# A delta-rule attention block with an expert layer: seven products for eight and eleven for twelve one block earlier, the weight sums by ScalarE copies and accumulating DMAs

## The chip, the cores and the metric

The kernel runs on one core of one Trainium2 chip. A core has a matrix engine (TensorE, PE in the profile), a vector engine (VectorE, DVE), an engine for activations (ScalarE, ACT), a general one (GpSimd, POOL), a sequencer that mostly issues transfers (SyncE, SP), and 16 DMA engines that all queues share. Each engine works off its own instructions in order and waits on semaphores for the others. The metric is the device time of one execution, in microseconds; the median over several runs counts.

## The reference

```python
# q, k, v: (4, 8, 768, 48); beta: (4, 8, 768)
k_n = k / (np.linalg.norm(k, axis=-1, keepdims=True) + 1e-06)
for t in range(S):
    y[:, :, t] = np.einsum('bhd,bhde->bhe', q[:, :, t], state)
    v_old = np.einsum('bhde,bhd->bhe', state, kt)
    state = state + bt[:, :, :, None] * np.einsum('bhd,bhe->bhde', kt, vt - v_old)
...
x = attn_out.transpose(0, 2, 1, 3).reshape(3072, 384)
h = x @ w_in                      # (384, 2048)
g = h * np.clip(h + 3.0, 0.0, 6.0) / 6.0
out = g @ w_out                   # (2048, 384)
```

## The kernel before

**Attention.** The 768 tokens are cut into 24 chunks of 32; the four batches stand side by side, so a chunk is 128 rows. For each chunk t there is a preparation (`prep`: POOL scales the keys by their inverse norms into kb, L510; PE turns kb and the queries, L524; ACT copies the turned tile, L532; PE forms the products sc, L547; DVE masks them into L and LB, L558, with masks mb that POOL makes, L486; POOL also makes bkb, L498), the inverse of a triangular matrix for a group of four chunks (`inverse`, the many small DVE operations of L759 and L764, ended by a transposition, L473), and the chain proper (`chain`: ks L806, R L901 and L909, pz and py L827, su L938, the update of the state L956, the output y L843, L819, L863, turned by PE, L873, and copied to xT, L877). `norms` prepares the inverse key norms of a group: squares (ACT for the first groups, POOL from the fourth on, L407 and L409), a DVE reduction each, L413, a root on ACT, L417, and small DVE operations up to L431, whose result L510 waits for.

**Expert layer.** Two chunks make a block of 256 tokens; there are 12 blocks, 0 to 11. For each block `up` forms h from xT and w_in, in 16 pieces of 128 columns of w_in, three matmuls of 256 columns each (L994), and ACT (L1001) and DVE (L1004) make g of each. `down` forms out from g and w_out: 32 matmuls of 384 columns (L1162) for a block.

From a certain block on, two cheaper schemes stand in for these. `down_by_seven` (from block `FIRST` = 2) cuts the matrices into quarters and forms out with seven products of quarters for eight (56 matmuls of 192 columns, L1226, in `product`); it needs sums of quarters of w_out (T1, T2, T4 in the tile `spare`, and a changed quarter B12 of w_out itself) and, per block, sums of quarters of g on DVE (L1212), copies of products on ACT (L1233) and additions on POOL (L1236). `up_by_eleven` (from block `UF` = 3) forms h with eleven products for twelve (L1066, nine matmuls for each of eight pieces, of 128 and 256 columns). It needs sums of quarters of w_in (S1, S2, S4 in the tile `sums_in`, and a changed W21 in w_in itself), sums of quarters of xT on DVE (`token_sums`, L1056), and additions on POOL (L1030) and DVE (L1093, L1097) to put g together.

**Sums of weights before.** `quarters` makes T1, T2 and T4 by twelve DVE operations (L1197), one at a time between other work, after the weights have been converted from their double-precision form (`convert`, last step L389); `last_quarter` changes B12 by four DVE operations (L1203) during `up` of block 2, drawn by `mlp_units`; `weight_sums` makes S1, S2, S4 and W21 by sixteen POOL operations (L1030) during `down` of block 1 and after.

**Order.** The first part is issued from a list of words, `ORDER`, written out by hand: each word takes the next step of a generator (`c` takes one of `convert` and then `quarters`; `u` one unit of the expert layer; `gu` one pending L1004; `n9` a step of the norms; `p9` of the preparation of chunk 9). After the list a loop over chunks takes a plan of 15 units a chunk; each unit takes one step of `mlp_units` and the attention's steps that the plan puts there. A block is 16 units of `up` and 16 of `down` (14 of `down_by_seven`). The order in which instructions are issued is the order on each engine's queue. PSUM tiles are handed out from a ring of four (`pm`) and one of two (`pc`), so a tile's last reader stands ahead of its next writer. The output tile o has one buffer.

SP issues the loads of keys, queries and values and the stores of o. POOL issues no DMA before the change.

Of the kernel before, what the change touches and what calls it, by code (L numbers as in the profile page):

```python
# [38 lines left out]
ru c i2 u*2 i2 gu i2*3 q i2*5 y4 h4 n9 i2 e*2 n9*2 i2*4 q i2 y4 e n9 u ru i2*3 u i2 ru*2 gu h4 u n9  # L39
i2*2 u i2 e i2*6 y4 u k n9*3 u gu i2 y4 n9 i2 p9 q i2*2 gu  # L40
# [4 lines left out]
def kernel(  # L45
# [21 lines left out]
    nc = tc.nc  # L67
# [950 lines left out]
    UF = 3  # L1018
# [13 lines left out]
    def weight_sums():  # L1032
        for j in range(0, NPR, 2):
            r = slice(j, j + 2)
            plus_minus(S1[:, r], W21[:, r], W22[:, r], ALU.add)
            yield
            plus_minus(S2[:, r], S1[:, r], W11[:, r], ALU.subtract)
            yield
            plus_minus(S4[:, r], W12[:, r], S2[:, r], ALU.subtract)
            yield  # L1040
            plus_minus(W21[:, r], W11[:, r], W21[:, r], ALU.subtract)
            yield
# [5 lines left out]
    def token_sums(blk):  # L1048
# [6 lines left out]
        for out, a, b in ((T1x, B12, B11), (T2x, B22, T1x), (B12, B22, B12), (T4x, B21, T2x)):  # L1055
            nc.vector.tensor_tensor(out=out, in0=a, in1=b, op=ALU.subtract)  # L1056
# [129 lines left out]
    FIRST = 2  # L1186
# [6 lines left out]
    def quarters():  # L1193

        for o, a, b in ((T1, B12, B11), (T2, B22, T1), (T4, T2, B21)):
            for f in range(0, HF, 2):
                nc.vector.tensor_tensor(  # L1197
                    out=o[:, f : f + 2], in0=a[:, f : f + 2], in1=b[:, f : f + 2], op=ALU.subtract
                )
                yield  # L1200

    def last_quarter(f):
        nc.vector.tensor_tensor(  # L1203
            out=B12[:, f : f + 2], in0=B22[:, f : f + 2], in1=B12[:, f : f + 2], op=ALU.subtract
        )

    def down_by_seven(blk):
# [12 lines left out]
        def product(n, a, b, half):  # L1220

            if half == 0:
                ring("pm", NPM, ("po", blk, "by", n))
                ps[n] = psM.tile([128, HM], FP32, name="po", tag=slot["pm"])
            for f in range(half * HF // 2, (half + 1) * HF // 2):
# [14 lines left out]
        settle()  # L1240
# [4 lines left out]
        yield  # L1245
        product(4, A22, T4, 0)
        yield
        product(4, A22, T4, 1)
        copy(C21, 4, -1.0)
        sums(ALU.add, A22, A21, A22, lo)  # L1250
        yield
        product(2, A12, B21, 0)
        sums(ALU.add, A22, A21, A22, hi)
        yield
        product(2, A12, B21, 1)
        copy(C11, 2)
# [6 lines left out]
        copy(C22, 5)  # L1263
# [33 lines left out]
    def mlp_units():  # L1297
# [10 lines left out]
        def downs(blk):  # L1308
            if blk >= FIRST:
                yield from down_by_seven(blk)  # L1310
                return
# [253 lines left out]
```

## Time and profile before

| what | us |
|---|---|
| median of three runs | 661.96 |
| lowest, highest | 661.61, 663.02 |
| span of the profiled execution | 660.3 |
| product of block 1 (`down`), start to end on PE | 148.07 to 178.76 |
| `up` of block 2 | 178.76 to 205.69 |
| seven products of block 2 | 205.69 to 230.00 |
| eleven products of block 3 | 230.00 to 255.78 |

The profile is of one execution, whose span is 1.7 us under the median. In timelines the first column is the start from the span's beginning and the second how long the piece took; a matmul in single precision leaves two records, so `x8` of L1162 is four matmuls. The bracket at the end is idle time of the engine before the piece and what ended it. In a table of windows the columns are length, then busy time and count of PE, PE's weight loads, DVE, ACT and POOL, the granted clock, the share of DMA and GB/s. The costliest groups of the expert layer:

```
L1066 PE MATMUL ph<-xT,w_in 128*128 128x128 f32 (+1 forms) x720 | 156.8, 321 | 0.0
L1226 PE MATMUL po<-w_out,g 128*128 128x192 f32 x640 | 110.6, 326 | 0.0
L994 PE MATMUL ph<-xT,w_in 128*128 128x128 f32 (+1 forms) x384 | 72.0, 338 | 0.6 <-ACT xT L877 0.6
L1162 PE MATMUL po<-w_out,g 128*128 128x384 f32 x128 | 45.4, 490 | 0.0
```

Columns: line, engine, operation, names, shapes, count; busy time and mean nanoseconds of one; idle time of the engine before them.

### The profile page before, as it was taken

What the parts mean: (1) busy time and instruction counts of PE and PEld (TensorE: products, weight loads), DVE (VectorE), ACT (ScalarE), POOL (GpSimd) and SP (SyncE); (2) the same over time, 40 slices, a digit from 0 to 9 for tenths busy, and PEclk for the clock granted to TensorE, in tenths of its full rate; (3) what the DMA queues carried; (4) which work ended last, traced back from release to release, by engine and by line L of the source; (5) the groups of instructions that cost most, each with busy time, mean ns of one, the idle gap of its engine ahead of it and who ended that gap; (6) DMA issues with size and microseconds to landing.
All of it is one profiled execution on the core that took longest, in us unless ns stands there. A gap on an engine that the chain in (4) does not pass through costs nothing.

```text
span 660.3 us, 26640 instructions
## 1 busy us (share of the span) xinstructions
PE 632.5 (96%) x11640; PEld 569.2 (86%) x11640; DVE 499.2 (76%) x1170; ACT 282.3 (43%) x548; POOL 225.1 (34%) x352
## 2 busy tenths in 40 slices
PE   2768999999999999999999999999999999999997
PEld 2658987776689989999999999999999999999997
DVE  5899877798657988758988848979658998456354
ACT  5887689332243154154154244244244144153250
POOL 6531022003661353553254354164051242331430
PEclk9998999999999999999999999999999999999999
DMA  7888346202040030041030030020020020000000
GB/s 174 204 198 235 77 102 164 51 25 43 9 87 18 3 74 3 3 90 22 3 74 3 2 74 3 2 63 2 3 50 2 3 49 3 23 18 2 26 1 24
DMA packets 88692, 33.28 MB, mean 50 GB/s; under 512 B 80224, under 2 KB 83424, under 8 KB 88576
## 3 DMA queue, kind: packets, MB, share of 16 engines
q1 hardware_dynamic: 88224, 31.29, 20.8%
q8 instruction: 91, 1.49, 0.9%
q10 hardware_dynamic: 352, 0.30, 0.2%
q14 instruction: 25, 0.20, 0.1%
HBM read 26.84 MB, written 4.72 MB: 48 GB/s over the span
## 4 chain that ended last, share of the span: by engine, by line
PE 91%; DVE 3%; DMA 2%; SPq 1%; ACT 1%; issue 1%; DVEq 0%
PE po L1226 28%; PE ph L1066 27%; PE ph L994 9%; PE po L1162 6%; PE ks L806 4%; PE su L938 3%; PE pt L524 3%; PE pz L827 3%; PE py L827 3%; PE sc L547 2%; PE yt L873 1%; DMA spare<-in_moe_w_in_dram 1%; PE pi L684 1%; DMA w_out<-in_moe_w_in_dram 1%; SPq L168 1%
## 5 line engine op out<-in xcount | busy, mean ns | idle before, releaser
L1066 PE MATMUL ph<-xT,w_in 128*128 128x128 f32 (+1 forms) x720 | 156.8, 321 | 0.0
L1030 POOL TENSOR_TENSOR g<-g 128x256 f32<-128x256 f32 (+1 forms) x144 | 88.6, 616 | 104.7 <-ACT g L1080 99.1
L1066 PEld LDWEIGHTS ph<-xT,w_in 128*128 128x128 f32 x720 | 116.8, 191 | 6.7
L1226 PE MATMUL po<-w_out,g 128*128 128x192 f32 x640 | 110.6, 326 | 0.0
L1226 PEld LDWEIGHTS po<-w_out,g 128*128 128x128 f32 x640 | 104.6, 190 | 0.5
L1080 ACT ACTIVATE g<-ph 128x512 f32<-128x512 f32 x72 | 43.1, 598 | 105.1 <-PE ph L1066 105.1
L1226 PE MATMUL po<-spare,g 128*128 128x192 f32 x480 | 86.7, 332 | 0.0
L1226 PEld LDWEIGHTS po<-spare,g 128*128 128x128 f32 x480 | 77.2, 190 | 1.8
L994 PE MATMUL ph<-xT,w_in 128*128 128x128 f32 (+1 forms) x384 | 72.0, 338 | 0.6 <-ACT xT L877 0.6
L1236 POOL TENSOR_TENSOR o<-o,u 128x192 f32<-128x192 f32 x18 | 13.3, 739 | 163.8 <-ACT o L1233 86.6
L994 PEld LDWEIGHTS ph<-xT,w_in 128*128 128x128 f32 x384 | 59.6, 195 | 7.7 <-ACT xT L877 0.8
L1093 DVE TENSOR_TENSOR g<-ph,g 128x256 f32<-128x256 f32 x72 | 30.2, 419 | 46.8 <-PE ph L1066 33.5
L759 DVE TENSOR_TENSOR pr<-A 128x30 f32<-128x30 f32 (+9 forms) x150 | 57.3, 382 | 3.3
L1212 DVE TENSOR_TENSOR g<-g 128x512 f32<-128x512 f32 x80 | 56.1, 722 | 3.5 <-PE po L1226 3.5
L1113 DVE SCALAR_TENSOR_TENSOR g<-o,g 128x512 f32<-128x512 f32 x72 | 52.6, 730 | 7.8 <-ACT o L1110 7.7
L764 DVE TENSOR_TENSOR A<-A,pr 128x30 f32<-128x30 f32 (+9 forms) x150 | 55.1, 367 | 3.3
L1110 ACT ACTIVATE o<-g,halves 128x512 f32<-128x512 f32 x72 | 52.2, 725 | 11.3 <-DVE g L1113 8.4
L1066 PE MATMUL ph<-beta_tok,sums_in 128*128 128x128 f32 x288 | 55.9, 275 | 0.0
L356 ACT ACTIVATE spare<-spare,places 128x768 uint16<-128x768 uint16 (+1 forms) x56 | 52.8, 947 | 3.2 <-DMA kf<-in_k_dram 1.6
L1233 ACT ACTIVATE o<-po 128x192 f32<-128x192 f32 x40 | 13.3, 332 | 82.7 <-PE po L1226 79.2
L510 POOL TENSOR_TENSOR kb<-kf,inv 128x384 f32<-128x384 f32 x24 | 21.7, 907 | 75.5 <-issue 43.1
L1162 PE MATMUL po<-w_out,g 128*128 128x384 f32 x128 | 45.4, 490 | 0.0
(141 smaller groups left out, 1019.1 us busy)
## 6 DMA issues: line engine op xcount, KB each, us to landing
kf<-in_k_dram SPq DMA_DIRECT2D x96, 48.0 KB, 2.6
qb<-in_q_dram SPq DMA_DIRECT2D x96, 48.0 KB, 2.4
vf<-in_v_dram SPq DMA_DIRECT2D x96, 48.0 KB, 2.1
out_dram<-o SPq DMA_DIRECT2D x90, 48.0 KB, 1.6
spare<-in_moe_w_in_dram SPq DMA_DIRECT2D x4, 768.0 KB, 6.6
w_out<-in_moe_w_in_dram SPq DMA_DIRECT2D x4, 768.0 KB, 6.1
w_out<-in_moe_w_out_dram SPq DMA_DIRECT2D x4, 768.0 KB, 5.8
spare<-in_moe_w_out_dram SPq DMA_DIRECT2D x4, 768.0 KB, 5.2
```

The lines of the kernel that those rows point to most:

```text
L356: nc.scalar.activation(out=z, in_=z if n else d.bitcast(I16)[:, :, :, 3], func=func, bias=places[:, n : n + 1], scale=scale,)
L759: nc.vector.tensor_tensor(out=pv, in0=A[:, j + 1 :, j].unsqueeze(2).to_broadcast([n, w, j]), in1=A[:, j, 0:j].unsqueeze(1).to_broadcast([n ...
L764: nc.vector.tensor_tensor(out=A[:, j + 1 :, 0:j], in0=A[:, j + 1 :, 0:j], in1=pv, op=ALU.subtract)
L994: nc.tensor.matmul(ph[:, cols], lhsT=w_in[:, s, f * 128 : (f + 1) * 128], rhs=xT[:, s, cols], start=(s == 0), stop=(s == NKT - 1),)
L1030: nc.gpsimd.tensor_tensor(out=out, in0=a, in1=b, op=op)
L1066: nc.tensor.matmul(ph[:, n], lhsT=w, rhs=x, start=start, stop=stop, skip_group_check=True)
L1080: nc.scalar.activation(out=gt, in_=ph[:], func=ACTF.Copy)
L1110: nc.scalar.activation(out=r, in_=g, func=ACTF.Relu, bias=half, scale=1.0 / 6.0)
L1113: nc.vector.scalar_tensor_tensor(out=g, in0=r, scalar=1.0, in1=g, op0=ALU.min, op1=ALU.mult)
L1162: nc.tensor.matmul(pos[c][:], lhsT=gs[blk, f // 2][:, f % 2, c * P : (c + 1) * P], rhs=w_out[:, f, :], start=(f == 0), stop=(f == NFC - 1),)
L1212: nc.vector.tensor_tensor(out=A(f, *out, 4), in0=A(f, *a, 4), in1=A(f, *b, 4), op=op)
L1226: nc.tensor.matmul(ps[n][:], lhsT=A(f - f % 2, *a)[:, f % 2], rhs=b[:, f], start=(f == 0), stop=(f == HF - 1),)
```

## The change

`FIRST` goes from 2 to 1 and `UF` from 3 to 2: block 1's product with w_out is made by seven products, block 2's with w_in by eleven. All sums of weights are made in another way: ACT copies one operand (with scale -1 where a sign is wanted, `minus`), and a DMA issued from POOL's queue adds the other one into it (`plus_by_dma`). Signs of some sums change so that every second step is an addition: T1 is B11 - B12, T1x is B11 - B12, and product 5 is copied with -1. T4 no longer goes through T2: it takes -B21, then B22, then T1. B12 and W21 are negated in place by ACT and then added to. In block 1 the order of the seven products is 1, 2, 4, 5, 7, 6, 3, with product 2 in four parts, so that the block has 16 units as before; in the other blocks it stays 1, 4, 2, 5, 7, 6, 3. Some `gu` and `c` words of `ORDER` move. The loop's branch for an ordinary `down` after block 0 goes.

There are nine such DMAs: T1, T4, T2 and T4 again (768 KB each), S1 (512 KB), B12 (768 KB), W21, S2 and S4 (512 KB each). On POOL's queue they stand, in this order, T1, T4, T2, T4, S1 and B12 ahead of kb (L510) and the masks of one chunk, W21 and S2 ahead of the next kb, bkb and masks, and S4, after one addition to o, ahead of the four L409. On ACT's queue the copies T1, T4 and T2 stand ahead of an L407 and the two evictions of block 0's po, and W21, S1 and B12 ahead of the root L417, S2 and S4 behind the copy of product 1.

```diff
-    UF = 3
+    UF = 2
...
     def weight_sums():
-        for j in range(0, NPR, 2):
-            r = slice(j, j + 2)
-            plus_minus(S1[:, r], W21[:, r], W22[:, r], ALU.add)
-            yield
...
+        minus(W21, W21)
+        minus(S1, W22)
+        yield
+        plus_by_dma(S1, W21)
+        nc.scalar.activation(out=S2, in_=W11, func=ACTF.Copy)
+        nc.scalar.activation(out=S4, in_=W12, func=ACTF.Copy)
+        for _ in range(4):
+            yield
+        plus_by_dma(W21, W11)
+        plus_by_dma(S2, S1)
+        for _ in range(4):
+            yield
+        plus_by_dma(S4, S2)
+        yield
...
-    FIRST = 2
+    FIRST = 1
...
     def quarters():
-        for o, a, b in ((T1, B12, B11), (T2, B22, T1), (T4, T2, B21)):
-            for f in range(0, HF, 2):
-                nc.vector.tensor_tensor(
-                    out=o[:, f : f + 2], in0=a[:, f : f + 2], in1=b[:, f : f + 2], op=ALU.subtract
-                )
-                yield
+        minus(T1, B12)
+        minus(T4, B21)
+        yield
+        plus_by_dma(T1, B11)
+        plus_by_dma(T4, B22)
+        nc.scalar.activation(out=T2, in_=B22, func=ACTF.Copy)
+        yield
+        plus_by_dma(T2, T1)
+        plus_by_dma(T4, T1)
+        past.add("quarters")
+        yield
+
+    def minus(out, a):
+        nc.scalar.activation(out=out, in_=a, func=ACTF.Copy, scale=-1.0)
+
+    def plus_by_dma(out, a):
+        nc.gpsimd.dma_start(out=out, in_=a, accum_op=ALU.add)
+
+    def last_quarter():
+        minus(B12, B12)
+        yield
+        plus_by_dma(B12, B22)
+        yield
...
+        if blk == FIRST:
+            for part in range(4):
+                product(2, A12, B21, part, 4)
+                if part == 3:
+                    copy(C11, 2)
+                yield
+            needs("quarters")
         product(4, A22, T4, 0)
...
-            for _ in downs(blk):
-                next(sums, None)
+            for n, _ in enumerate(down_by_seven(blk)):
                 next(sums, None)
+                if blk == FIRST:
+                    next(b12, None)
                 yield
```

More of the change, by code (lines that the diff above doesn't have):

```diff
@@ L1307, in mlp_units @@
                 yield
[L1308 to L1311, printed above, removed]
[L1312 to L1317 removed]
+        b12 = last_quarter()
         for blk in range(1, N // CB):
```

60 lines of the change are left out of this document (25 added, 35 removed).

## The prediction

> **What bounds the kernel now.** I read the page first, for the engine that the chain of waits runs through, then the stages that the change touches, and then each engine's timeline around them.
>
> ```profile
> PE 632.5 (96%) x11640; PEld 569.2 (86%) x11640; DVE 499.2 (76%) x1170; ACT 282.3 (43%) x548; POOL 225.1 (34%) x352
> PE 91%; DVE 3%; DMA 2%; SPq 1%; ACT 1%; issue 1%; DVEq 0%
> ```
>
> TensorE (PE) is the bound: 91% of the chain is its own work, and no other engine is near full over the span. So every matmul that goes from the dense part comes off the end, and every wait put before a matmul there goes on it. The stages by windows (the ordinary product of block one, the ordinary `up` of block two, the seven products of block two, the eleven of block three):
>
> ```profile
> 148.07:178.76 30.69, 30.69 (x543) 20.00 (x542) 23.50 (x58) 7.37 (x15) 13.57 (x17) 1.00 0.12 25
> 178.76:205.69 26.93, 26.93 (x433) 23.14 (x428) 17.70 (x42) 9.60 (x20) 15.05 (x21) 1.00 0.36 69
> 205.69:230.00 24.31, 24.31 (x444) 23.24 (x443) 20.69 (x48) 4.79 (x11) 4.57 (x7) 1.00 0.01 2
> 230.00:255.78 25.78, 25.78 (x478) 23.41 (x477) 21.43 (x53) 12.85 (x26) 14.51 (x23) 1.00 0.24 49
> ```
>
> The first figure after the length is PE's busy time: it equals the length, so PE never waits here. What feeds PE in these stages stands in the timelines; these lines of PE, DVE, POOL and ACT carry the argument:
>
> ```profile
> 148.06 2.74 PE L1162 MATMUL po<-w_out,g 128*128 128x384 f32 x8
> 156.12 0.60 PE L524 MATMUL pt<-ident,kb 128*128 128x128 f32 x4
> 169.78 0.89 PE L938 MATMUL su<-R,bkb 32*64 32x48 f32 x64
> ```
>
> ```profile
> 154.41 0.35 DVE L431 RECIPROCAL inv<-nt 128x32 f32<-128x32 f32 x1
> 168.37 0.41 DVE L558 TENSOR_TENSOR LB<-sc,mb 128x256 f32<-128x256 f32 x1
> ```
>
> ```profile
> 154.89 0.83 POOL L510 TENSOR_TENSOR kb<-kf,inv 128x384 f32<-128x384 f32 x1 [43.06 <-issue]
> 164.97 0.82 POOL L409 TENSOR_TENSOR sq<-kf 128x384 f32<-128x384 f32 x1
> ```
>
> ```profile
> 140.35 0.51 ACT L407 ACTIVATE sq<-kf 128x384 f32<-128x384 f32 x1
> ```
>
> Two chains end close to PE. The norm chain: DVE's L431 at 154.41 lets POOL make kb (done 155.72), and PE turns kb at 156.12, 0.4 us later. The square chain: POOL's first L409 at 164.97 starts four squares and their DVE reductions in turn; DVE runs L558 between them (ends 168.78) and PE's su, which needs it, comes at 169.78, 1.0 us later.
>
> **The change part by part.** All times are on the clock of the trace before.
>
> *Matmuls.* Eight records of 384 columns (two a matmul) take 148.06 to 150.65, 0.65 us a matmul; 32 of them are 20.7 us. The last block's 56 matmuls of 192 columns take 18.2 us. So the product of block one loses 2.5 us of PE. The `up` stage of 26.93 us becomes one like those of eleven, 25.78 (230.00 to 255.78) and 25.58 (280.08 to 305.66): 1.25 us less. Together 3.75 us, if nothing waits.
>
> *The norm chain.* DVE is busy without a gap from 130 to 156, so block one's matmuls don't set when L431 comes. It comes later: one more L1004 (0.34 us) stands ahead of it, and ACT's three copies T1, T4, T2 stand ahead of the L407 of 140.35. A copy of 1536 costs 1.46 us (0.60 for 512 and 0.33 for 192 give 0.84 ns an element), three 4.2: that L407 ends at 145.1, its reduction on DVE starts at 145.15 instead of 144.62, 0.5 us later. So L431 starts at 155.3, kb ends at 156.5, and PE, which would be there at 154.4 (0.25 us of that for po's buffers, evicted later behind the same copies), waits until 156.55. The wait eats 2.1 us of the 2.5; after it only one short piece (half of product 2's last half, 0.65 us) is still to be won. The other ACT copies (W21, S1, B12, S2, S4: 1.03, 1.03, 1.46, 1.03, 1.03) run to 154.7; the ACT work behind them, root for L420 (152.3, wanted at 154.4) and the xT eviction, has cover.
>
> *The removed sums.* DVE's twelve L1197 and four L1203 (0.5 to 0.9 us each) and POOL's sixteen `sums_in`/`w_in` operations (0.73) go, DVE gains eight L1212 (0.69) and POOL sixteen L1030 on g and five L1236. PE waited for none of them, and waits for none now: nothing.
>
> *Nine accumulating DMAs on POOL's queue.* In POOL's order: T1, T4 (first pass), T2, T4 (second), S1, B12, then kb and mb, W21, S2, then kb, bkb, mb, one L1236, S4, then the four L409. An issue waits on POOL for what it reads, so T2 waits for T1's landing, second T4 for the first, W21 for S1, S4 for S2, and everything behind waits too. The trace has no POOL DMA and no accumulation. Their price is bounded by plain packets:
>
> ```profile
> spare<-in_moe_w_out_dram SPq DMA_DIRECT2D x4, 768.0 KB, 5.2
> out_dram<-o SPq DMA_DIRECT2D x90, 48.0 KB, 1.6
> ```
>
> The packet records give 121 ns for 3072 bytes, 25 bytes/ns an engine, 16 engines: 768 KB (T's and B12) move in 1.95 us, 512 KB (S's, W21) in 1.3. A 48 KB store whose bytes take 0.1 us lands after 1.6, so 1.5 is fixed. One end is this plain price; the other is twice the bytes, since each sum reads its destination as well as its source through the same engines. I take twice, 3.9 and 2.6: two plain packets are the nearest rows to two operands read. By 36 ns for a 768-byte packet, the pieces of T1, T4 and B12, it is 4.6 for those: the upper end.
>
> The Trainium skill, Collectives: The Full Stack, section The bandwidth ceiling, says that a reduction by DMA runs at half a copy's rate because it needs two source reads (its ratio 1.93). No run here shows it yet; by 1.93 instead of 2 the 27.3 us of movement below shrink by 1.0 us, and the sum would be 664.9.
>
> On one queue, one behind the other: T1 issues at 142.0 (its ACT copy's end), moves to 145.9, lands 147.4; T4 to 149.8, lands 151.3; T2 to 153.7; second T4 (issued 151.3) to 157.6, lands 159.1; S1 (151.7) to 160.2, lands 161.7; B12 to 164.1, lands 165.6; W21 (161.7) to 166.7; S2 to 169.3, lands 170.8. PE wants T4 at 158.1 (156.55 and 0.44 + 0.65 + 0.44): 1.0 us of wait. B12 is wanted at 167.6: no wait. But S4 is issued only at 170.8, and takes POOL 0.4 (the SP's issue of 768 KB, 385 to 452 ns, is the nearest row). So the first L409 starts at 171.2, not 164.97; 3.8 us later (as 164.97 to 168.78) L558 ends, at 175.0, and su starts 5.2 us later than before.
>
> *Sum.* From su on PE runs as before, then wins 1.25 in the eleven: 660.3 + 5.2 - 1.25 = 664.3 for a profiled execution. The median of the runs shown lies 1.65 above its span (661.96 against 660.3): **665.9 us**, slower by 0.6%. With 4.6 for the pieces of 768 bytes and the same doubling for 512-byte ones (26 ns between the records of 192 and 768 bytes, so 3.3) S2 lands at 174.3, su starts 8.8 late: 669.5. With 1.75 times the plain price S2 lands at 167.4, su is 1.8 late: 662.5. So the forecast's own range is 662.5 to 669.5; it decides from the factor at which S2 lands after 165.7, where POOL would get to S4 anyway: about 1.65.
>
> **The rivals.**
>
> *The sums move at the plain rate* (the second read hides beside the write). Then T4 lands at 151.3 and S2 at 162.1 (at 1.5 times still at 163.9), before POOL gets to S4 at 165.7 (L558's end at 163.7, mb 1.4, L1236 0.6). The square chain starts at 166.1, su at 169.9, 0.1 late; the eleven gives 1.25: 660.8, not slower, at the edge of what can be told. For it: DMA is only 0.12 busy in this stage, while the 5.2 us of the plain row were taken under the load of the first 120 us. Against: each byte written is two to read.
>
> *All 3.75 us are won*: 658.2. It needs the norm chain 2 us earlier; against it stands DVE without a gap up to 156. For it, PE is all there is on the chain afterwards.
>
> *POOL's issuing is the price*, not the bytes. T1, T4, S1, B12 and W21 are 1024 pieces each. If POOL makes pieces at the pace of its elements (0.73 us for 256, L1030) that is 2.9 us each: S1 issues from 151.0 to 153.9, B12 to 156.8, kb ends at 157.6 and PE turns it 1.1 late; W21 and S2 then push POOL's S4 to 166.9 and, with plain bytes, su to 171.1, 1.3 late, less 1.25: 662.0, no change.
>
> **How the numbers follow.** Forecast 0.45; plain rate 0.30; all won 0.12; issuing 0.08; 0.05 for what I don't see, mostly slower. About 0.2%, 1.3 us, is what a measurement can tell, so faster is under 660.6: all won and a little over half of the plain rate, 0.30. Same: the rest of the plain rate and the issuing, 0.17. Slower 0.53. The range that holds all but 2 in 10 runs from 658.0 (all won) to 670.5 (the dear packets and a microsecond): cases of both signs, beside the 662.5 to 669.5 of the likeliest.
>
> **What would show it.** In the profile after: PE idle before kb's transpose (about 2 us, released by POOL's L510), before product 4 (1 us, by the DMA into `spare`), and most before su (5 us, released by L558, POOL's L409 behind the last accumulating DMA). The DMA section gives the landing of 768 KB: near 3.5 us says plain, 5.5 and over twice. If POOL's own rows of these DMAs are long, it is the issuing. A span under 658 would make the norm chain wrong; landings of 10 us and more would make it far slower than I say.

## The result, and the profile after

| what | before | after |
|---|---|---|
| median of four runs each, us | 662.36 | 685.53 |
| lowest to highest | 661.61 to 663.02 | 681.11 to 685.95 |
| span of the profiled execution | 660.3 | 683.8 |
| su behind the ordinary or new product of block one, start | 169.78 | 187.85 |
| `up` or eleven of block two, length | 26.93 | 26.22 |

The change makes the kernel slower, by a ratio of 1.0335 (95% interval 1.0306 to 1.0365). The forecast was 665.9, with a range up to 670.5: the side was right, the size was not. The page of the changed kernel, its busy time of PE and its chain of waits:

```profile
PE 635.3 (93%) x11736; PEld 580.4 (85%) x11736; DVE 501.2 (73%) x1176; ACT 295.2 (43%) x567; POOL 236.9 (35%) x366
PE 86%; DMA 5%; DVE 3%; POOL 2%; SPq 1%; issue 1%; ACT 1%; POOLq 0%; DVEq 0%
```

PE's share of the chain fell from 91 to 86%, and POOL, which was not on it, is there with 2%. Where PE stands still is told by its timeline. These are its waits between 140 and 275 us that last over 0.5 us; all but the last end in a line that the change touches or feeds:

```profile
151.76 1.57 PE L1246 MATMUL po<-w_out,g 128*128 128x192 f32 x8 [0.81 <-DVE g L1004]
162.84 1.11 PE L524 MATMUL pt<-ident,kb 128*128 128x128 f32 x4 [7.58 <-POOL kb L510]
174.38 0.66 PE L524 MATMUL pt<-ident,kb 128*128 128x128 f32 x4 [1.52 <-POOL kb L510]
187.85 1.19 PE L938 MATMUL su<-R,bkb 32*64 32x48 f32 x60 [7.17 <-DVE LB L558]
269.35 0.31 PE L827 MATMUL py<-R,LB 32*32 32x48 f32 x9 [1.68 <-issue]
```

The kb of 162.84 and the su of 187.85 (60 of its 64 records; four stand ahead of the wait) are two of the three places that the forecast named, with 2.1 and 5.2 us; at the third, product 4, PE does not wait. The last line is of another kind: PE stops in the middle of a group of small matmuls, and nothing in the profile releases it. What keeps POOL from kb and from the squares is in its own timeline:

```profile
141.89 3.31 POOL L1219 DMA_DIRECT2D spare<-w_out  x2 [30.32 <-ACT spare L1216]
151.08 0.89 POOL L1219 DMA_DIRECT2D spare<-spare  x1 [5.88 <-ACT sums_in L1216]
157.93 0.85 POOL L1219 DMA_DIRECT2D spare<-spare  x1 [5.96 <-DMA spare<-w_out]
158.48 1.89 POOL L1219 DMA_DIRECT2D sums_in<-w_in  x1
159.38 2.55 POOL L1219 DMA_DIRECT2D w_out<-w_out  x1
160.29 2.49 POOL L510 TENSOR_TENSOR kb<-kf,inv 128x384 f32<-128x384 f32 x1
170.99 1.56 POOL L1219 DMA_DIRECT2D w_in<-w_in  x1 [7.07 <-PE pz L827]
182.87 0.86 POOL L1219 DMA_DIRECT2D sums_in<-sums_in  x1 [6.08 <-DMA sums_in<-sums_in]
183.49 1.10 POOL L409 TENSOR_TENSOR sq<-kf 128x384 f32<-128x384 f32 x1
```

In order: T1 and T4, T2, T4's second pass, S1, B12, kb, W21 (S2 stands right behind it), S4, the first square. The bracket of W21 names a PE instruction, but S1's landing, at 170.45 by its semaphore, is what it stood for. From 151.97 to 157.93 POOL stands at T4's second pass, until the first has landed (157.64); kb was ready to be made at 155.1. From 176.78 to 182.87 it stands at S4, until S2 has landed (182.58), and the squares stand behind it. The issues themselves take some 0.9 us where rows are whole (each partition's bytes lie in one piece) and some 1.6 where they are cut into pieces of 768 or 512 bytes. Rows of queued POOL work overlap, so the time from the end of one to the end of the next is what counts: T4's, S1's and B12's end at 158.8, 160.4 and 161.9, and kb's at 162.8. The DMA section gives the landings:

```profile
spare<-w_out POOLq DMA_DIRECT2D x2, 768.0 KB, 11.5
spare<-spare POOLq DMA_DIRECT2D x2, 768.0 KB, 9.3
sums_in<-sums_in POOLq DMA_DIRECT2D x2, 512.0 KB, 7.6
w_out<-w_out POOLq DMA_DIRECT2D x1, 768.0 KB, 17.7
sums_in<-w_in POOLq DMA_DIRECT2D x1, 512.0 KB, 12.0
w_in<-w_in POOLq DMA_DIRECT2D x1, 512.0 KB, 9.1
```

These contain the time in the queue. From 144.18, when the first byte moves, to 182.22, when S2's last one does, the queue is never empty for over 0.1 us: by the packets' own times, 16 engines need 37.2 us for the first eight sums, where the forecast had 27.3. Last, the windows of four stages and stretches (length; busy time and count of PE, its weight loads, DVE, ACT and POOL; granted clock; share of DMA; GB/s):

```profile
147.85:198.37 50.52, 33.34 (x592) 30.17 (x591) 23.93 (x61) 12.97 (x23) 22.81 (x27) 0.83 0.83 129
198.37:224.59 26.22, 26.05 (x481) 23.77 (x477) 16.65 (x40) 12.93 (x26) 14.05 (x23) 1.00 0.40 76
187.85:191.60 3.75, 3.75 (x128) 3.54 (x129) 3.03 (x6) 0.32 (x1) 2.66 (x4) 0.50 0.02 4
270.10:273.50 3.40, 3.40 (x15) 3.21 (x15) 1.09 (x3) 1.49 (x3) 1.18 (x2) 0.50 0.02 5
```

The stage of block one's product takes 50.52 us for 30.69, with 17.2 us of it idle. The two last windows are stretches in which PE works at half its clock: the granted clock is 0.50 from 184.77, within the wait before su, to 191.59, and from 270.10, 0.8 us behind the pause at 269, to 273.51 (and from 157.46 to 167.70 around the wait before kb). So the 23.5 us between the two spans add up from the end that counts: su starts 18.1 later; 3.75 us at clock 0.50 behind it cost 1.9; the eleven of block two gives back 0.7; the pause of 1.68 at 269 and the 3.40 us at half clock behind it cost 3.4, and another such pause, 1.02 us at 315, makes 23.7. The two waits before kb are not in this sum: S2's landing sets su, and they lie in front of it.

### The profile page after: what moved, and what is told of

It is laid out like the page before. It is cut to its first block, busy times and chain, and to the rows that moved or that the text cites. A ratio compares the mean times of both kernels' runs of the same rounds, so it can differ in the third digit from the quotient of the medians.

```text
span 683.8 us, 26908 instructions
## 1 busy us (share of the span) xinstructions
PE 635.3 (93%) x11736; PEld 580.4 (85%) x11736; DVE 501.2 (73%) x1176; ACT 295.2 (43%) x567; POOL 236.9 (35%) x366
## 4 chain that ended last, share of the span: by engine, by line
PE 86%; DMA 5%; DVE 3%; POOL 2%; SPq 1%; issue 1%; ACT 1%; POOLq 0%; DVEq 0%
PE ph L1074 29%; PE po L1246 29%; PE ph L994 6%; PE pt L524 3%; PE ks L806 3%; PE po L1170 3%; PE su L938 3%; PE py L827 3%; PE pz L827 3%; PE sc L547 2%; DMA sums_in<-sums_in 2%; PE yt L873 1%; DMA out_dram<-o 1%; DMA w_out<-in_moe_w_in_dram 1%; DMA spare<-in_moe_w_in_dram 1%
## 5 line engine op out<-in xcount | busy, mean ns | idle before, releaser
L1030 POOL TENSOR_TENSOR g<-g 128x256 f32<-128x256 f32 (+1 forms) x160 | 97.8, 612 | 123.1 <-ACT g L1088 116.8
L1246 PE MATMUL po<-w_out,g 128*128 128x192 f32 x704 | 123.1, 328 | 0.8 <-DVE g L1004 0.8
L1246 PEld LDWEIGHTS po<-w_out,g 128*128 128x128 f32 x704 | 115.4, 191 | 1.9 <-DVE g L1004 1.1
L1246 PE MATMUL po<-spare,g 128*128 128x192 f32 x528 | 96.8, 335 | 0.1
L1246 PEld LDWEIGHTS po<-spare,g 128*128 128x128 f32 x528 | 86.2, 192 | 2.5 <-ACT o L1253 0.5
L1232 DVE TENSOR_TENSOR g<-g 128x512 f32<-128x512 f32 x88 | 61.8, 723 | 12.3 <-PE po L1246 12.3
L1121 DVE SCALAR_TENSOR_TENSOR g<-o,g 128x512 f32<-128x512 f32 x80 | 58.7, 733 | 8.9 <-ACT o L1118 8.9
L1118 ACT ACTIVATE o<-g,halves 128x512 f32<-128x512 f32 x80 | 57.8, 723 | 12.9 <-DVE g L1121 9.7
L1074 PE MATMUL ph<-beta_tok,sums_in 128*128 128x128 f32 x320 | 62.2, 276 | 0.0
L759 DVE TENSOR_TENSOR pr<-A 128x30 f32<-128x30 f32 (+9 forms) x150 | 58.4, 389 | 3.6
L764 DVE TENSOR_TENSOR A<-A,pr 128x30 f32<-128x30 f32 (+9 forms) x150 | 53.2, 355 | 3.1
L1074 PEld LDWEIGHTS ph<-beta_tok,sums_in 128*128 128x128 f32 x320 | 48.8, 193 | 0.0
L532 ACT ACTIVATE KQ<-pt 128x512 f32<-128x512 f32 x48 | 28.2, 598 | 34.7 <-PE pt L524 33.8
```

The source lines that it names most:

```text
L759: nc.vector.tensor_tensor(out=pv, in0=A[:, j + 1 :, j].unsqueeze(2).to_broadcast([n, w, j]), in1=A[:, j, 0:j].unsqueeze(1).to_broadcast([n ...
L764: nc.vector.tensor_tensor(out=A[:, j + 1 :, 0:j], in0=A[:, j + 1 :, 0:j], in1=pv, op=ALU.subtract)
L1030: nc.gpsimd.tensor_tensor(out=out, in0=a, in1=b, op=op)
L1074: nc.tensor.matmul(ph[:, n], lhsT=w, rhs=x, start=start, stop=stop, skip_group_check=True)
L1118: nc.scalar.activation(out=r, in_=g, func=ACTF.Relu, bias=half, scale=1.0 / 6.0)
L1121: nc.vector.scalar_tensor_tensor(out=g, in0=r, scalar=1.0, in1=g, op0=ALU.min, op1=ALU.mult)
```

## The experiments

Kernels that differ only from 140 us on (on PE's queue from 148) still reach the same su at different times, between 144.3 and 148.5: it is the fifth su of the profile, at 144.3 in the changed kernel and 144.6 before, and the expectations call it chunk 5. So beside the median a "tail" is given: the span less the start of that su. It is 515.7 before and 539.5 after, good to 0.1 us. A tail is of one execution; how much it varies between executions of one kernel was not measured.

**One half of the change at a time.** The first kernel takes `weight_sums` and `token_sums` of the change and UF = 2, with FIRST = 2 and the sums of w_out on DVE (cut where dots stand, as in all edits here):

```diff
-    UF = 3
+    UF = 2
...
-            plus_minus(S1[:, r], W21[:, r], W22[:, r], ALU.add)
+        plus_by_dma(S1, W21)
```

> Kernel before with block two's product with w_in by eleven and the four sums of w_in by ScalarE copies and accumulating DMAs; block one's product with w_out stays ordinary and its sums stay on VectorE. Theory (each accumulating DMA moves slowly, 4.2 us for 512 KB in 512-byte pieces and 2.8 in whole rows, and they move one behind the other): with an empty queue ahead S1 lands near 156, S2 near 167, POOL comes to S4 only 0 to 2 us late, so at most 2 us of wait before su and none before kb's transposition beyond 1 us: 661 to 664 us. Rival (POOL's own time for issuing, 0.9 to 1.7 us a DMA, is the price): the same 4 of 9 issues stand ahead of the same work, so 4/9 of the loss of 23 us, near 672. Rival (whatever runs beside the DMAs gets slower): the DMAs move 2 of 5.9 MB, near 670.

The second is the changed kernel with UF = 3 and `weight_sums` and `token_sums` as before:

```diff
-    UF = 2
+    UF = 3
```

> Changed kernel with block two's product with w_in made in the ordinary way again and the sums of w_in by POOL operations in block two; the five accumulating DMAs of w_out and the seven products of block one stay. Theory: T4 still lands near 157.6, POOL still stands at the second T4 until then, kb ends near 161 and PE waits some 6 us before kb's transposition, then runs about 3 us at half clock; no S2, so no wait before su: 662.4 - 2.5 + 6 + 2 = 668, 666 to 671. If e1 is near 662 and this near 668, the two halves together (685.5) cost 17 us more than the sum of both, because S1, W21 and S2 stand behind w_out's DMAs. Rival (POOL's issuing): 5/9 of 23 us, near 675.

Measured: 672.7 (671.2 to 675.0) and 673.0 us (671.5 to 674.7), ratios 1.0141 (1.0100 to 1.0181) and 1.0143 (1.0104 to 1.0182); tails 525.5 and 524.8. Both miss high, and both medians lie near what the rival of POOL's issuing gave (672 and 675); the waits show another cause. PE's timeline, with w_in alone and with w_out alone:

```profile
178.38 1.19 PE L938 MATMUL su<-R,bkb 32*64 32x48 f32 x60 [3.06 <-DVE LB L558]
```

```profile
163.45 1.12 PE L524 MATMUL pt<-ident,kb 128*128 128x128 f32 x4 [6.02 <-POOL kb L510]
```

With w_in alone S1 lands at 161.30 and S2 11.7 us later, at 172.97; POOL stands at S4 for 5.4 us until then, and su waits 3.1. A pause of 1.9 comes in a group of sc, and PE works 5.7 us at half clock. With w_out alone PE waits 6.0 before kb and 1.7 at product 4, and works 3.2 us at half clock. The halves cost 9.8 and 9.1 in the tail, together 18.9, of the whole 23.8: 4.9 us more than their sum, and not the 17 that were expected.

**What of the DMA is dear.** First the same bytes in whole rows:

```diff
-        plus_by_dma(T1, B11)
-        plus_by_dma(T4, B22)
+        plus_by_dma(T1, w_out[:, 0:4])
+        plus_by_dma(T4, w_out[:, 8:12])
...
-        plus_by_dma(S1, W21)
+        plus_by_dma(S1, w_in[:, 0, 1024:2048])
```

(and W21 and B12 likewise).

> Changed kernel; the accumulating DMAs T1, T4, B12, S1, W21 take the same number of bytes, but from and to whole stretches of 6144 or 4096 bytes a partition instead of 768- or 512-byte pieces. That adds other parts of the weights than the sums need (T1, T4, B12, S1, W21 get other values). Theory (small pieces cost 84 ns for 768 bytes and 65 for 512, against 530 for 6144 and 340 for 4096): 768 KB take 4.2 us instead of 5.7, 512 KB 2.8 instead of 4.2; T4 lands near 154.8, S2 near 174.5; the wait before kb shrinks from 7.6 to 4 us, that before su from 7.2 to 2 to 3, less time at half clock: near 675, 672 to 678. If the price went by bytes alone: 685. If all small-piece cost were the loss: under 668.

Then plain copies:

```diff
-        nc.gpsimd.dma_start(out=out, in_=a, accum_op=ALU.add)
+        nc.gpsimd.dma_start(out=out, in_=a)
```

> Changed kernel, its nine DMAs as plain copies on the same queue, in the same order and with the same pieces; nothing is added, so T1, T2, T4, B12, S1, S2, S4, W21 hold one operand instead of a sum. Theory (it is the accumulation in the DMA engines that moves slowly): a 768-byte piece takes 36 to 45 ns instead of 84 to 91, T4 lands by 150, S2 by 166, no wait over 1.5 us before kb or su: 661 to 664. Rival (POOL's issuing, 0.9 to 1.7 us a DMA, or its waiting on one landing after another, whatever the kind): 680 or more. Rival (any SBUF to SBUF transfer is as slow): 680 or more with pieces at 80 ns.

Measured: whole rows 681.4 us (ratio 1.0262, 1.0217 to 1.0307; tail 534.7), plain copies 666.65 (1.0065, 1.0039 to 1.0090; tail 521.5). The number of issues and their order on POOL's queue are the same in all three, so 19 of the 23 us come with the accumulation. Part of this is POOL's time: the issue of a cut DMA takes it 1.6 us with accumulation and 0.9 as a plain copy, that of whole rows 0.9 and 0.55. The packets' records, means:

```
                          bytes   ns      768 or 512 KB take
changed   cut rows, 768     768   90.9    5.8 us
          cut rows, 512     512   66.4    4.2
          whole rows       6144   529     4.2
          whole rows       4096   343     2.7
plain     six of 768       4608   236     2.5
          whole rows       6144   259     2.1
          rows and eights of 512
                           4096   204     1.6
```

Accumulating costs 1.7 to 2.0 times a plain copy in whole rows and 2.3 to 2.6 times in cut ones: by the sizes of the packets, a plain copy packs six pieces of 768 bytes or eight of 512 into one, an accumulation moves each by itself. Whole rows bring T4 down to 154.63 and S2 to 177.24, but PE still waits 2.2 before kb, 3.0 at product 4 and 5.2 before su, and the pause at 265 with its half clock stays, so less comes back than expected. With plain copies the two waits are nearly as the rival of the forecast had them. The landings are later than it said: T4's second pass lands at 158.69 for 151.3 and S2 at 168.42 for 162.1, and only 1.8 us of each is this profile's later fifth su.

```profile
spare<-w_out POOLq DMA_DIRECT2D x2, 768.0 KB, 6.3
spare<-spare POOLq DMA_DIRECT2D x2, 768.0 KB, 5.4
w_out<-w_out POOLq DMA_DIRECT2D x1, 768.0 KB, 8.7
```

```profile
158.16 0.66 PE L524 MATMUL pt<-ident,kb 128*128 128x128 f32 x4 [0.86 <-POOL kb L510]
169.21 0.83 PE L547 MATMUL sc<-KQ 64*32 64x64 f32 x62 [1.20 <-issue]
173.44 0.97 PE L938 MATMUL su<-R,bkb 32*64 32x48 f32 x60 [0.36 <-DVE LB L558]
```

(DMA section and PE's timeline of the kernel with plain copies.) Both waits are under a microsecond. Its tail is 5.8 us over that of the kernel before, and three pauses of the kind without a releaser make 5.6 of it: 1.20 here, 1.94 at 254 with 1.7 lost at half clock behind it, and 0.73 at 300.

**The pauses.** They were counted in PE's instructions: matmuls, weight loads (a single-precision matmul is two of each) and the few that only wait for a semaphore. The 18 profiles of this study leave 58 pauses of over 0.25 us, past 60 us of the span, without a releaser. All lie at 193 or 194 modulo 256, and in each case a 16 KB packet on the queue of kind `instruction` began 2.2 to 2.9 us before PE went on. The changed kernel has 92 such packets for 23671 instructions of PE, one for 256. Over all 18 traces PE goes past such a count 1638 times with a packet before it, and never sooner than 2.16 us after the packet for it (counts and packets taken in order) began. To move them, small matmuls into a tile that is overwritten were put at the start of PE's program, four instructions each:

```diff
             pt = psM.tile([128, NP, P], FP32, name="pt", tag=slot["pm"])
+            for _ in range(14 if t == 0 and j == 0 else 0):
+                nc.tensor.matmul(
+                    pt[0:32, 0, 0:64], lhsT=ident[0:64, 0:32], rhs=ident[0:64, 0:64], start=True, stop=True
+                )
```

A first try used `lhsT=ident[:]` and `rhs=ident[:, 0:32]` into 128 rows:

> Changed kernel with 14 small matmuls more at the very start of TensorE's program, where it waits for its first keys. A single-precision matmul is four instructions there, so all that follows stands 56 instructions later. In the runs so far every pause of TensorE that nothing in the profile explains came when 193 or 194 instructions modulo 256 had been issued (1.68 us at 269, 1.02 us at 315 in the changed kernel). Theory (code is loaded in blocks of 256 instructions, and a block that holds two bursts of small attention matmuls is used up before the next is there): the shift takes the block's border out of those bursts; both pauses go, and with the first the 3.4 us at half clock behind it: 685.5 - 1.7 - 1.0 - 1.7 = 681, 679 to 683. Rival (the pauses hang on data or on transfers beside): unchanged, 685.

> Kernel before with 50 small matmuls more at the very start of TensorE's program, 200 instructions, as many as block one's and block two's new products add in the changed kernel (201). Theory of code blocks: the borders then fall in the later chunks where they fall in the changed kernel, and pauses of 1 to 2 us come there, with or without a stretch at half clock: 664 to 667. Rival (pauses hang on the DMAs or the waits of the changed kernel): 662.5, no change; the 50 matmuls lie in TensorE's idle start.

then the form above, 14 in the changed kernel and 50 in the kernel before:

> As the kernel with 56 instructions more, but with 14 matmuls of 64 rows and 64 columns, which are over before the first keys are there (in the first try each of the 14 took 0.2 us and held up the start). Theory of code blocks: from chunk 5 on the same gain as there, 4.1 us (535.4 from that point to the end, against 539.5 in the changed kernel): 681.4 us, 680 to 683. Rival: 685.5.

> Kernel before with 200 instructions more at the start, in matmuls of 64 rows and 64 columns that are over before the first keys are there. Theory of code blocks: two pauses, 1.6 us in a burst near 250 and 1.1 near 295, as in the first try (518.7 us from chunk 5 to the end against 515.7): 662.4 + 3.0 = 665.4, 664.5 to 667.5, with up to 1.7 more if the first is followed by half clock. Rival: 662.5, no change.

Measured: 692.0 and 684.2 us in the first form, 691.4 (ratio 1.0436, 1.0409 to 1.0462) and 674.3 (1.0153, 1.0124 to 1.0183) in the second. None of the four medians came out as expected. A matmul took 0.43 us in the first form and 0.22 in the second, not the 0.2 of the expectation, so 50 of them run 15.4 and 4.7 us past the first keys (8.1) and hold up the start; 14 do not. But in the changed kernel 56 instructions put borders into groups of small matmuls in the first 110 us: in the second form pauses of 1.57 and 2.93 come at 87 and 106, and the fifth su at 154.7 for 144.3. The tails are as expected in both forms: 535.4 and 534.9 for the changed kernel (539.5 without), 518.7 and 518.7 for the kernel before (515.7 without). In the kernel before, which has no such pause past 60 us, 200 instructions bring two behind the fifth su, at the same counts as in the changed one (PE's timeline, second form):

```profile
259.42 0.29 PE L831 MATMUL py<-R,LB 32*32 32x48 f32 x9 [1.62 <-issue]
303.95 0.30 PE L551 MATMUL sc<-KQ 64*32 64x64 f32 x2 [1.04 <-issue]
```

So these pauses belong to the place in the program, not to the DMAs: the change adds 201 instructions and takes them on itself, 4.4 us with the half clock. The Trainium skill, Runtime: NRT & Kernel Launch, section Instruction fetch mechanics, has code come in blocks of 16 KiB, 256 instructions, by the sequencer's own DMA, and the cost of crossing a border "mostly hidden". Block and packet agree with the rows above; hidden it was not in the 58 pauses, of up to 3.4 us. Two groups of 64 small matmuls at a border do not always bring one: in the kernel before, su and py from 397.2 to 398.8 fill a whole block without one; the next block's packet had begun 2.5 us before its border. That the loading makes the pause is inferred from the counts, the packets and the 2.16 us; why a packet begins late was not looked into.

The kernel with plain copies and 56 instructions more:

> The kernel with plain copies in the place of the accumulating DMAs (T1, T2, T4, B12, S1, S2, S4, W21 hold one operand), with 56 instructions more at the start. Theory: what plain copies still lost (5.8 us from chunk 5 on) is all code blocks, 1.9 and 1.2 and 0.7 us of pauses and 1.7 at half clock; with the borders moved 661 to 662.5 is left, the forecast's own price for the plain rate (660.8). Rival (nine DMAs on POOL's queue cost some us even at the plain rate): 664 and more.

Measured 673.2 us, ratio 1.0151 (1.0129 to 1.0173): the early pauses again (fifth su at 154.3). Its tail is 518.3, 3.2 less than without and 2.6 over the kernel before; pauses of 0.36 and 0.26 and waits of 0.87 before kb, 1.33 at product 5 (for DVE's sums of g, L1236) and 0.97 before su are in it. So even with landings as early as a plain copy's the change did not reach the 515.7 less 3.75 that its matmuls promise: by the tail the rival is nearer than the theory.

**Half clock.** The wait before kb was filled with work, 33 matmuls of 128 columns into the tile that the transposition overwrites, and 31 small ones at the start make up a full block:

```diff
+            if t == 9 and j == 0:
+                for n in range(33):
+                    nc.tensor.matmul(
+                        pt[:, n % NP], lhsT=ident[:], rhs=w_in[:, 2, 0:128], start=True, stop=True
+                    )
```

> Changed kernel with 33 matmuls of 128 columns, into the tile that kb's transposition then overwrites, ahead of the transposition that waits 7.6 us, so that TensorE is busy in that wait; and 31 small ones at the start, so that 256 instructions are added in all and code borders stay where they were from there on. Theory (the wait costs twice: the idle time, and then a clock of 0.5 until 167.7): the clock stays at 1.00 through 157 to 168, the 4.9 us that TensorE worked at half clock become 2.5 shorter: 683, 682 to 684, with the wait itself (until kb, 162.8) unchanged and the pauses at 269 and 315 still there. Rival (the half clock costs nothing because the next thing, S2, sets the time anyway): su still starts at 187.9 and the time stays at 685.5.

Measured 697.6 us, ratio 1.0521 (1.0498 to 1.0545), with the start held up as above (fifth su at 160.7); tail 536.5. The clock stays at 1.00 up to kb, but PE then waits for T4 at product 4 and for S2's landing before su (PE's timeline):

```profile
182.66 4.52 PE L1256 MATMUL po<-spare,g 128*128 128x192 f32 x16 [2.09 <-DMA spare<-spare]
203.87 1.19 PE L948 MATMUL su<-R,bkb 32*64 32x48 f32 x60 [6.00 <-DVE LB L568]
```

This su starts 43.1 us after the fifth su (43.5 in the changed kernel). The rival was right: the half clock in front of su costs next to nothing, S2 sets su. The 3.0 us in the tail are not a gain of this: there is no pause at the place of 269.

**No DMAs at all.** S1, S2, S4, T1, T2, T4 and W21 by POOL, B12 by DVE:

```diff
-        plus_by_dma(T1, B11)
+        plus_minus(T1, B11, B12, ALU.subtract)
...
-        plus_by_dma(T2, T1)
-        plus_by_dma(T4, T1)
+        plus_minus(T2, B22, T1, ALU.add)
+        plus_minus(T4, T2, B21, ALU.subtract)
```

> Changed kernel without its DMAs and ScalarE copies: S1, S2, S4 and then T1, T2, T4 are made by POOL operations in POOL's idle time from 111 to 155 (8.8 and some 13 us), B12 by four VectorE operations and W21 by four POOL operations in block one. Theory (all of the loss stands on the accumulating DMAs, the algorithm itself is worth its 3.75 us less the wait for the norm chain): T4 is there at 153, kb at 156.3, PE waits 1.5 to 2 us there and nowhere else: span 658 to 661, median 660 to 663; code pauses as in the changed kernel may add 2.7 to 4.4. Rival (seven and eleven one block earlier cost TensorE or VectorE more than they save): 668 and more.

Measured 680.9 us, ratio 1.0265 (1.0230 to 1.0299); the theory's 660 to 663 fell. The fifth su comes at 153.0, 8.4 late, before any of the new products has run. DVE and POOL in that stretch:

```profile
132.90 3.40 DVE L759 TENSOR_TENSOR pr<-A 128x130 f32<-128x130 f32 x1
136.33 0.30 DVE L764 TENSOR_TENSOR A<-A,pr 128x130 f32<-128x130 f32 x1
147.49 3.54 DVE L764 TENSOR_TENSOR A<-A,pr 128x240 f32<-128x240 f32 x1
```

```profile
132.69 3.45 POOL L1030 TENSOR_TENSOR spare<-w_out 128x1536 f32<-128x1536 f32 x1
147.27 3.49 POOL L1030 TENSOR_TENSOR spare<-w_out,spare 128x1536 f32<-128x1536 f32 x1 [11.12 <-issue]
```

A DVE operation on two tiles that starts under a POOL operation of 1536 elements ends with it, after 3.4 and 3.5 us for 0.3 and 0.4; the inverse's many L759 and L764 are of this kind, and DVE has no idle time over 0.04 us from 130 to 156 in the kernel before. The Trainium skill, SBUF — State Buffer, section SBUF: two separate sides, says that VectorE and GpSimd share a port pair that one holds for a whole instruction while the other is blocked. The rows agree. So POOL's idle time there is no cover for sums. The tail, 527.7, is 12 us longer too: PE waits 4.3 us at 161 for y (L863), which stands behind the same late DVE operations, and 2.4 before su. The rival (the new products cost more than they save) is not refuted by this kernel, as DVE's delay hides what they would do alone.

The eleven alone, its sums by POOL as before but from the last five units of block one (before the change they stand from 182.6 to 218.8, later than the description above puts them):

```diff
-    UF = 3
+    UF = 2
...
-                next(sums, None)
-                next(sums, None)
+                for _ in range(4 if n >= 11 else 0):
+                    next(sums, None)
```

> Kernel before with UF = 2 alone: block two's product with w_in by eleven, its sums of w_in by the same sixteen POOL operations as before, drawn from the last five units of block one (behind the second square of L409). No DMA, no ScalarE copy, block one's product with w_out ordinary. Theory: the eleven saves 1.25 us, nothing waits, and code borders fall as in the kernel with w_in alone (0.8 us near 470, and in the burst near 168): 661.2, up to 663 with the pauses. Rival (POOL's operations slow VectorE or push a kb back): 664 and more. If it is 661 or less it beats both kernels.

Measured 670.0 us, ratio 1.0106 (1.0085 to 1.0126), tail 522.1: slower, as its rival said. POOL's sums stand ahead of the third and fourth square, DVE's y (L863) behind the reductions of these, and PE waits 3.07 us for y at 178.9 and 1.31 at 208.6.

**Order on POOL's queue.** The changed kernel with W21 and S2 behind kb of the next chunk and S4 behind the squares:

```diff
-        for _ in range(4):
+        for _ in range(7):
             yield
         plus_by_dma(W21, W11)
         plus_by_dma(S2, S1)
-        for _ in range(4):
+        for _ in range(5):
             yield
```

> Changed kernel, same operations, but W21's and S2's DMAs are issued from POOL's queue behind kb of chunk 10 and S4's behind the four squares of L409. Theory (su waits because POOL, which must make the squares, stands in front of S4's DMA until S2 has landed; the data of S4 are not wanted before the eleven): the first L409 starts near 177 instead of 183.5, su near 181.5 instead of 187.9, the wait before kb of chunk 10 (1.5 us) goes, and with the waits most of the 1.9 us at half clock behind su: 685.5 - 1.5 - 6.5 - 1.9 = 675.6, 674 to 678. Rival (the time is set by when S2 and S4 are there, so the wait only moves to the eleven): PE waits 5 to 7 us at the first product with S4 and the time stays at 683 to 686.

Measured 678.4 us, ratio 1.0232 (1.0203 to 1.0262), tail 530.8: 8.7 of the 23.8 come back (7.2 of the 23.2 by the medians), by nothing but order. PE's timeline:

```profile
164.67 1.11 PE L524 MATMUL pt<-ident,kb 128*128 128x128 f32 x4 [6.73 <-POOL kb L510]
183.50 0.71 PE L938 MATMUL su<-R,bkb 32*64 32x48 f32 x45 [0.90 <-DVE LB L558]
```

The wait before su is 0.90 for 7.17; the one before kb, now the bound, stays. S4 lands at 191.2 and nobody waits for it. Then kb, too, ahead of the second passes, with S1 and B12 behind them:

```diff
-ru c*2 i2 u*2 c i2 gu ... i2 e*2 c n9*2 ... i2 p9 q i2*2
+ru c*2 i2 u*2 c i2 gu ... i2 e*2 n9*2 ... i2 p9 q c i2*2
...
         minus(S1, W22)
-        yield
+        for _ in range(6):
+            yield
         plus_by_dma(S1, W21)
...
         minus(B12, B12)
-        yield
+        for _ in range(6):
+            yield
         plus_by_dma(B12, B22)
```

> As the kernel with W21, S2 and S4 later on POOL's queue, and kb of chunk 9 ahead of the second passes T2 and T4, with S1 and B12 behind those. Theory (here, other than before su, it is the sum itself that is late: T4's second pass cannot start before its first has landed, 158 to 159, and needs 5 us): PE turns kb on time but waits 4 to 6 us at product 4 in place of 6.7 before kb: 675 to 679. Rival (only the order on POOL's queue is the price): no wait over 2 us there, 670 and less.

Measured 678.3 us, ratio 1.0235 (1.0202 to 1.0269), as without. PE's timeline:

```profile
160.31 0.66 PE L524 MATMUL pt<-ident,kb 128*128 128x128 f32 x4 [0.87 <-POOL kb L510]
171.34 4.24 PE L1248 MATMUL po<-spare,g 128*128 128x192 f32 x16 [9.28 <-DMA spare<-spare]
```

The wait moves from kb to product 4, and is 9.3 us, longer than the 4 to 6 expected: T2's pass is issued only behind kb, at 160.2 (153.6 in the kernel above), and moves ahead of T4's, which lands at 171.2. Here the sum itself is late.

**The DMAs where there is time.** FIRST = 2 and UF = 2, all nine sums by copies and accumulating DMAs; T1's and T4's first passes at the start of block two's eleven, then, in a second kernel, ahead of it and with T4's second pass before T2's (the second kernel's main edit):

```diff
+                if blk + 1 == FIRST and n >= 12:
+                    if n == 12:
+                        drain(rest)
+                        quarter = quarters()
+                    next(quarter, None)
```

> Kernel before with UF = 2 and FIRST = 2: block two's product with w_in by eleven, block one's product with w_out ordinary, all nine sums by ScalarE copies and accumulating DMAs, spread out: S1 at block one's start, W21 and S2 behind kb, S4 behind the squares, T1 and T4 at the start of block two's eleven, their second passes and B12 near its end, so that POOL never stands before a landing. Theory (the DMAs cost nothing where there is time for them and nothing queued behind): 662.4 - 1.25 = 661.2, and 0.8 to 2.7 more where a code border falls into a burst: 661 to 664. Rival (POOL's issuing, or ScalarE's copies, or the DMAs' traffic cost by themselves): 666 and more.

> As the kernel with all nine DMAs spread out, but T1's and T4's DMAs stand ahead of block two's eleven (their ScalarE copies in block one), T4's second pass in its middle and B12 after it, so that no kb stands behind them and T4 is there 8 us before product 4 of block two. Theory (DMAs in time cost nothing): the waits of 4.6 and 3.9 us go, and the half clock behind them (5.7 us of TensorE's work in the two stretches, 2.8 lost): 678.6 - 8.5 - 2.8 = 667.3, with 2.2 of pauses at code borders still in it: 664 to 668. Rival (the DMAs' traffic or POOL's issuing costs by itself): 672 and more.

Measured 678.6 us (1.0229, 1.0204 to 1.0254) and 667.1 (1.0052, 1.0035 to 1.0069). In the first, POOL's two issues stand ahead of a kb at 192 (4.6 us of wait) and T4 is 3.9 late; its time is on its rival's side. In the second, with tail 519.3, these are PE's longest waits between 140 and 275:

```profile
169.73 0.63 PE L547 MATMUL sc<-KQ 64*32 64x64 f32 x37 [2.12 <-issue]
194.51 0.86 PE L547 MATMUL sc<-KQ 64*32 64x64 f32 x64 [0.61 <-ACT y L843]
201.88 0.80 PE L827 MATMUL py<-R,LB 32*32 32x48 f32 x56 [0.43 <-issue]
```

With a pause of 0.69 at 473, pauses make 3.2 of its 3.6 us over the kernel before. The DMAs move as slowly as in the changed kernel (91 and 72 ns a piece), and cost next to nothing; here they serve block two, as block one's product is the ordinary one. No kernel of the study is faster than the one before.

## Why the prediction was wrong in size

*Where and how: right in the main.* PE is stopped most before su, by L558 behind POOL's squares behind an accumulating DMA: the chain of the forecast, step for step. It is stopped at kb by POOL too, though for another reason (below). That the sums taken off DVE and POOL are worth nothing was not tested by itself; no kernel shows a gain from it.

*The step that failed* is the size of one term, "I take twice, 3.9 and 2.6: two plain packets are the nearest rows to two operands read", with the moves that start at the issue. Three sums of 768 KB in 768-byte pieces took 5.8 us each and not 3.9, two of 512 KB in 512-byte pieces 4.2 and not 2.6; in whole rows they took 4.2 and 2.7, near the forecast. The first byte moved 2.3 us after the first issue. Eight sums took 37.2 for 27.3, and S2 landed at 182.58 for 170.8. From there it goes as predicted but for 1.1 us, su at 187.85 for 175.0: 12.9 of the 19.5 us between the two spans (683.8 and 664.3). The upper end, 4.6 and 3.3, was worked out from the right thing, a packet of 768 bytes, but doubled a plain packet of that size; a small piece accumulated is 84 ns in the median and 91 in the mean for the 72 of that rule. Its plain rows, 36 and 121 ns, are medians too: their means are 40 and 151, and twice these is 5.1 and 4.8 us for 768 KB. The ratio of two that the Trainium skill, Collectives: The Full Stack, gives to a reduction (1.93 there) agrees with whole rows of 6144 bytes here, 529 against 259 ns, less with those of 4096 (1.7); for pieces it is 2.3 and 2.6.

*Two terms that the sum did not have.* PE's clock is 0.50 for 3.4 us or a multiple in and after the long waits: 1.9 behind su. And pauses at borders of code blocks, with the half clock behind one of them: 4.4. The rest is the eleven, which gave 0.7 and not 1.25.

*The norm chain and POOL's issue.* The forecast had kb wait for the norm chain. L431 ran at 154.76 (forecast 155.3), but kb was 6.3 us later than forecast, since T4 landed at 157.64 for 151.3 and three issues of 0.9 to 1.6 us, for 0.4 assumed, stood between. So POOL, standing at T4's landing, made this wait, and not the norm chain; the 1.0 us at product 4 went under in it. The wait is covered by the one before su; the order experiments show that it is the next bound, at about the same place.

*The rivals.* That the sums move at the plain rate would have given 660.8: with plain copies the waits are nearly as that rival said, the median is 666.65 and the tail, less its pauses, 0.2 over the kernel before. POOL's issuing as the whole price does not fit: the waits before kb and su end with landings, and with plain copies, as many and in the same order, they are under a microsecond. But an issue of a cut accumulating DMA costs POOL 1.6 us, half of that rival's 2.9 and 0.7 more than a plain one, and no run separates this part from the slower movement. All 3.75 us won was not seen in any kernel. The forecast's own sign for more, "landings of 10 us and more would make it far slower than I say", is what came: 11.5 and 17.7.

*Open.* Why profiles differ by up to 4 us at the fifth su when nothing was changed ahead of it; what the new products would bring with sums that cost nothing, as every kernel that has them lost time elsewhere; and where the last 2 us of the tail of the kernel with plain copies and 56 instructions more lie.

## What to carry to other kernels

Price an accumulating DMA by its pieces: here 12 bytes a ns and engine in whole rows and about 8 in pieces of 512 or 768, where a plain copy moves 20 to 24; and put every instruction that others wait for ahead of an issue that must wait for a landing, which alone brought back 8.7 of 23.8 us. Where one sum must land before the next can start, an earlier start helped: in the kernel where every sum was there before it was wanted, the same DMAs cost next to nothing. Differences of up to 10 us came with nothing but 56 instructions more ahead, so compare two kernels behind the same point of their profiles before a mechanism is named.

## What the runs showed of the hardware that was not expected

PE stopped for 0.3 to 3.4 us at some of the borders of 256 instructions, 58 times in 18 profiles, and never went past one sooner than 2.16 us after a 16 KB packet of code began; 56 instructions more at the start moved the fifth su by 10 us in the changed kernel and 8 in the one with plain copies. Around waits of 3.0 to 9.3 us the granted clock was 0.50 for 3.4 to 10.2 us, and for 3.4 behind the pause of 1.7 in a stretch of small matmuls, but not behind one of 2.1 in the kernel with all DMAs earlier. A plain copy by POOL's queue joined pieces into packets of 4096 and 4608 bytes, an accumulating one kept them at 512 and 768. And a DVE operation of 0.4 us lasted 3.5 under a POOL operation.
